# First q projection moved ahead of the second chunk's layer norm, with the first chunk's norm split over two engines

## The chip, the cores and the metric

The kernel runs on one core of one Trainium2 chip. The metric is the device time of one execution in microseconds (us), the median of three runs. The core has a matrix engine (PE; its weight loads are shown apart as PEld), a vector engine (VectorE, DVE in the profile), a scalar engine (ScalarE, ACT), GpSimd (POOL), and a sync engine (SP) that queues most of the transfers. All take their instructions in a fixed order that was decided when the kernel was built.

## The reference

The input x has 2048 tokens of 1024 features. It is normalized per token, then goes through a local attention (32 heads of 32, 8 keys at a distance of 2) and through a gated MLP, and both are combined with x:

```python
xn = _layernorm(x)                         # (x - mean) / sqrt(var + 1e-5), per token
qkv = xn @ wqkv                            # 1024 -> 3 x 1024: q, k, v
logits[w] = q[s] . k[s - 2 w] * Dh**-0.5   # w = 0..7
s = (softmax(logits) @ v[s - 2 w]) @ wo
g = silu((silu(xn @ w1) * (xn @ w3)) @ w2) # 1024 -> 3584 -> 1024
out = x + s * g
```

Data are bf16.

## The kernel before

The tokens are worked on in four chunks of 512 (CH), two chunks to a block (BL = 1024). A chunk is four tiles of 128 tokens. Each is loaded with tokens on partitions, normalized, and transposed by PE against an identity matrix; the transposed tiles are copied from PSUM into xT, which holds two chunks. The projections and the MLP read xT. The MLP's products are done by a scheme with sums of blocks (`xn_sums`, `w_sums`), which needs xT of both chunks of a block.

The norm comes in two forms. `ln_norm` takes the statistics on DVE and only the square root on ACT; `ln_norm_act` does the sums, squares and the scaling on ACT and only two tiny operations on DVE. In the kernel before, the first form serves block 0, the second block 1:

```python
def ln_norm(c, sts, xt4):
    ...
    for i, st in enumerate(sts):
        nc.sync.dma_start(out=xt4[:, st, :], in_=x_flat[g * P:(g + 1) * P, :])
        for h in range(2):
            nc.vector.bn_stats(out=stats[:, h, :], in_=xt4[:, st, h * 512:(h + 1) * 512])
        nc.vector.bn_aggr(out=mv[:, i, :], in_=stats[:])
    nc.scalar.activation(out=rstd[:], in_=mv[:, :, 1], func=ACTF.Sqrt, bias=eps_t[:], scale=1.0)
    nc.vector.reciprocal(out=rstd[:], in_=rstd[:])
    for i, st in enumerate(sts):
        nc.vector.tensor_scalar(out=xt4[:, st, :], in0=xt4[:, st, :], scalar1=mv[:, i, 0:1],
                                scalar2=rstd[:, i:i + 1], op0=ALU.subtract, op1=ALU.mult)

def ln_norm_act(c, sts, xt4):
    ...
    for i, st in enumerate(sts):
        nc.sync.dma_start(out=x_t, in_=x_flat[g * P:(g + 1) * P, :])
        nc.scalar.activation(out=junk[:], in_=x_t, func=ACTF.Copy, scale=-1.0 / D, accum_out=v[:, 0, i:i + 1])
        nc.scalar.activation(out=junk[:], in_=x_t, func=ACTF.Square, bias=v[:, 0, i:i + 1], accum_out=v[:, 1, i:i + 1])
    nc.scalar.activation(out=v[:, 2], in_=v[:, 1], func=ACTF.Sqrt, bias=eps_t[:], scale=1.0 / D)
    with tc.high_priority():
        nc.vector.reciprocal(out=v[:, 2], in_=v[:, 2])
        nc.vector.tensor_mul(v[:, 3], v[:, 0], v[:, 2])
    for i, st in enumerate(sts):
        nc.scalar.activation(out=x_t, in_=x_t, func=ACTF.Identity, bias=v[:, 3, i:i + 1], scale=v[:, 2, i:i + 1])

def ln_tp(c, st, xt4):                       # 8 transposes and 2 copies for one tile
    for kh in range(2):
        tp = bank(f"tp{c}_{st}_{kh}")        # one of 8 PSUM banks
        for k in range(KH):                  # KH = 4
            nc.tensor.matmul(tp[:, k * P:(k + 1) * P], lhsT=xt4[:, st, kt * P:(kt + 1) * P], rhs=ident[:], ...)
        nc.scalar.copy(out=xT[:, c % 2, kh * KH:(kh + 1) * KH, st * P:(st + 1) * P], in_=tp[:]...)

def ln_transpose(c, group=2):
    xt4 = r8.tile([P, NST, D], BF16, tag="r8", name=f"x{c}")    # one of 6 buffers of 8 KB a partition
    for st0 in range(0, NST, group):
        ln_norm(c, range(st0, st0 + group), xt4)
        for st in range(st0, st0 + group):
            ln_tp(c, st, xt4)

def qkv(c):
    ...
    for t in range(3):                       # q, k, v
        for hf in range(2):
            wt = r8.tile([P, 4, D], BF16, tag="r8")
            nc.sync.dma_start(out=wt[:], in_=wqkv_r[:, hf * 4:(hf + 1) * 4, t * D:(t + 1) * D])
        for j in range(NJ):                  # 8 groups of 8 matmuls, 128x512 each
            ps = bank(f"qkv{c}_{t}_{j}")
            mm_prod(ps, ...)                 # reads xT[:, half], all 512 tokens
            with tc.high_priority():
                nc.scalar.copy(out=dst, in_=ps[:])

ln_transpose(0, group=1)
ln_transpose(1)
for b in range(NB):
    qkv(c0)                                  # c0 = 2 b
    ...
    xn_sums(); mlp_up(...); attention(c0); ...; qkv(c1); mlp_up(...); attention(c1); mlp_down(b); wo(c0)
```

At the very start, 12 matmuls on a tile of zeros keep PE busy while the first tile of x is on its way.

Of the kernel before, what the change touches and what calls it, by code (L numbers as in the profile page):

```python
# [1 line left out]

# [14 lines left out]
def kernel(  # L17
# [21 lines left out]
    nc = tc.nc  # L39
# [8 lines left out]
    NST = CH // P  # L48
# [67 lines left out]
    def mm_prod(ps, lhs, rhs, first):  # L116
        n = len(lhs)
        for k in range(n):
            nc.tensor.matmul(  # L119
                ps[:], lhsT=lhs[k], rhs=rhs[k], start=(first and k == 0),  # L120
                stop=(k == n - 1), skip_group_check=not first,
            )

    def bank(name):
        return psum.tile([P, CH], FP32, tag="mm", name=name)
# [13 lines left out]
    def ln_norm(c, sts, xt4):  # L139
        n = len(sts)  # L140
        mv = small.tile([P, n, nc.vector.BN_AGGR_DIM], FP32, tag="mv")
        rstd = small.tile([P, n], FP32, tag="rstd")
        for i, st in enumerate(sts):
            g = c * NST + st
            nc.sync.dma_start(out=xt4[:, st, :], in_=x_flat[g * P:(g + 1) * P, :])
            stats = small.tile([P, 2, nc.vector.BN_STATS_DIM], FP32, tag="stats")
# [6 lines that stand above are left out]
            nc.vector.tensor_scalar(  # L153
                out=xt4[:, st, :], in0=xt4[:, st, :], scalar1=mv[:, i, 0:1], scalar2=rstd[:, i:i + 1],
                op0=ALU.subtract, op1=ALU.mult,
            )
# [16 lines left out]
            x_t = xt4[:, st, :]  # L173
            nc.scalar.activation(out=x_t, in_=x_t, func=ACTF.Identity, bias=v[:, 3, i:i + 1], scale=v[:, 2, i:i + 1])

    def ln_tp(c, st, xt4):
        for kh in range(2):
            tp = bank(f"tp{c}_{st}_{kh}")
            for k in range(KH):
                kt = kh * KH + k  # L180
                nc.tensor.matmul(
                    tp[:, k * P:(k + 1) * P], lhsT=xt4[:, st, kt * P:(kt + 1) * P], rhs=ident[:],
                    start=(k == 0), stop=(k == KH - 1), skip_group_check=True,
                )
            nc.scalar.copy(
                out=xT[:, c % 2, kh * KH:(kh + 1) * KH, st * P:(st + 1) * P],
                in_=tp[:].rearrange("p (k t) -> p k t", k=KH),
            )

    def ln_transpose(c, group=2):  # L190
        xt4 = r8.tile([P, NST, D], BF16, tag="r8", name=f"x{c}")
        for st0 in range(0, NST, group):
            ln_norm(c, range(st0, st0 + group), xt4)
            for st in range(st0, st0 + group):
                ln_tp(c, st, xt4)

    def qkv(c):
        half = c % 2
        if c > 0:
            nc.gpsimd.tensor_copy(out=kT[:, :, 0:HALO], in_=kT[:, :, CH:CH + HALO])  # L200
            nc.gpsimd.tensor_copy(out=vT[:, :, 0:HALO], in_=vT[:, :, CH:CH + HALO])  # L201
        for t in range(3):
            wts = []
# [3 lines that stand above are left out]
                wts.append(wt[:].rearrange("p k (c j) -> p k j c", j=NJ))  # L207
            for j in range(NJ):
                ps = bank(f"qkv{c}_{t}_{j}")
                mm_prod(ps, [wts[kt // 4][:, kt % 4, j, :] for kt in range(KT)],  # L210
                        [xT[:, half, kt, :] for kt in range(KT)], True)
                if t == 0:
                    dst = qo[:, half, j, :]
                elif t == 1:
                    dst = kT[:, j, HALO:HALO + CH]
                else:
                    dst = vT[:, j, HALO:HALO + CH]
                with tc.high_priority():
                    nc.scalar.copy(out=dst, in_=ps[:])  # L219

    def tree(t, z, op):
        op(t[:], z[:, 0:4, :], z[:, 4:8, :])
        op(t[:, 0:2, :], t[:, 0:2, :], t[:, 2:4, :])
        op(t[:, 0:1, :], t[:, 0:1, :], t[:, 1:2, :])
# [61 lines left out]
    def xn_sums():  # L286

        k_1, k_2 = slice(0, KH), slice(KH, KT)
        with tc.high_priority():
            nc.vector.tensor_sub(xs[:, 0], xT[:, 1, k_1, :], xT[:, 0, k_1, :])  # L290
            nc.vector.tensor_sub(xs[:, 1], xT[:, 1, k_2, :], xs[:, 0])
            nc.vector.tensor_sub(xs[:, 2], xT[:, 1, k_2, :], xT[:, 1, k_1, :])
            nc.vector.tensor_sub(xs[:, 3], xT[:, 0, k_2, :], xs[:, 1])
# [7 lines left out]
    def flush():  # L301
        while pend:
            pend.pop(0)()
# [101 lines left out]
    def w2_load(i):  # L405
        nc.sync.dma_start(out=w2_quarters(i).rearrange("p (a c) n -> p a c n", a=2), in_=w2_q[:, i])
# [15 lines left out]
    def mlp_down(b):  # L422
# [81 lines left out]
        for st in range(NST if b + 1 < NB else 0):  # L504
            ln_tp(2 * b + 2, st, xn[0])
# [7 lines left out]
        for st in range(NST if b + 1 < NB else 0):  # L513
            ln_tp(2 * b + 3, st, xn[1])
# [7 lines left out]
    def wo(c):  # L522
        u = c % 2
        gt = gts[u]
        for dh in range(2):
            wot = r8.tile([P, NJ, CH], BF16, tag="r8")
            nc.sync.dma_start(out=wot[:], in_=wo_r[:, :, dh * CH:(dh + 1) * CH])
            cols = slice(dh * CH, (dh + 1) * CH)
            for st in range(NST):
                g0 = (c * NST + st) * P  # L530
                ps = bank(f"s{c}_{dh}_{st}")
                mm_prod(ps, [qo[:, u, j, st * P:(st + 1) * P] for j in range(NJ)],
                        [wot[:, j, :] for j in range(NJ)], True)
                x_e = k2.tile([P, 2, CH], BF16, tag="k2")
                nc.sync.dma_start(out=x_e[:, 0], in_=x_flat[g0:g0 + P, cols])
                o_t = k2.tile([P, CH], FP32, tag="k2")
                with tc.high_priority():
                    nc.vector.tensor_mul(o_t[:], ps[:], gt[:, dh * NST + st])  # L538
                    nc.vector.tensor_add(x_e[:, 1], o_t[:], x_e[:, 0])  # L539
                    nc.scalar.dma_start(out=out_flat[g0:g0 + P, cols], in_=x_e[:, 1])  # L540

    cut = (11, 10)
    ln_transpose(0, group=1)
    ln_transpose(1)
    for b in range(NB):
        c0, c1 = 2 * b, 2 * b + 1
        qkv(c0)
        if b == 0:
            w2_load(0)
        else:  # L550
            wo(c0 - 1)
        xn_sums()
        mlp_up(b, range(cut[b]))
        attention(c0)
        flush()
        qkv(c1)
        mlp_up(b, range(cut[b], FB))
        flush()
        attention(c1)
        mlp_down(b)  # L560
        wo(c0)
# [31 lines left out]
```

## Time and profile before

| | |
|---|---|
| median of 3 runs | 779.67 us (778.84 to 781.32) |
| span of the profiled execution | 777.5 us |
| PE busy | 750.1 us (96%), 3457 matmuls |
| DVE busy | 602.0 us (77%) |
| ACT busy | 319.6 us (41%) |
| granted PE clock, mean | 0.982 |
| first q matmul | 21.74 us |
| first k matmul | 37.58 us |

How to read the profile: "busy" is the time in which an engine has at least one instruction under way. The page gives shares over the whole span, and under them the span in 40 slices with a digit for the busy tenths of each. For a change that touches the first tens of microseconds the whole-span shares say little; the same numbers for short windows, the timeline of single instructions, and the chain of work that ended last say more. The clock column is the share of PE's full clock that was granted. In names such as tp_2_0_180 the first two numbers are the token tile and the half of the features, the last only a running number; qkv_0_3 is q's fourth group, qkv_1 is k and qkv_2 is v. x_125 is the x buffer of chunk 0, x_214 that of chunk 1. L181 is the line of the transposes, L185 that of their copies, L119 that of all other matmuls, L148 to L153 the norm on DVE, L166 to L174 the norm on ACT.

### The profile page before, as it was taken

The numbers are of one execution on the slowest core, as the hardware profiler recorded it, in microseconds if no ns is written. First come the engines' busy times: TensorE is split into PE (matmuls) and PEld (weight loads), VectorE is DVE, ScalarE is ACT, GpSimd is POOL, SyncE is SP. The second block draws the span as 40 slices with busy tenths as digits, with TensorE's granted clock in tenths as the row PEclk, the third lists the DMA queues.
The fourth block names the chain that finished last, engine by engine and source line by source line (L and its number), as shares of the span: only waits on it lengthen the run. The fifth ranks groups of instructions, "written<-read, shape, count | busy, mean of one in ns | idle before, by whom it ended". The sixth has DMA issues, their size and how long they took to land.

```text
span 777.5 us, 9339 instructions
## 1 busy us (share of the span) xinstructions
PE 750.1 (96%) x3457; PEld 377.0 (48%) x3516; DVE 602.0 (77%) x829; ACT 319.6 (41%) x531; POOL 97.2 (12%) x172
## 2 busy tenths in 40 slices
PE   5999999999799999999999989999999999999997
PEld 3665444444365444445466434444456544444443
DVE  7249997896999899341599999474995995934997
ACT  4335444464134479456033045464433444221200
POOL 0000024124000000504000002221000004040000
PEclk7899999999999999999999989999999999999999
DMA  9362679889835395748863634756554347564634
GB/s 330 109 196 69 212 237 326 275 252 320 301 134 161 125 316 196 216 159 249 283 187 118 217 118 163 223 152 192 150 162 168 130 143 201 184 176 162 188 105 141
DMA packets 123117, 150.56 MB, mean 194 GB/s; under 512 B 6080, under 2 KB 97728, under 8 KB 119488
## 3 DMA queue, kind: packets, MB, share of 16 engines
q1 hardware_dynamic: 110336, 115.36, 47.8%
q0 software_dynamic: 8128, 30.42, 11.6%
q10 hardware_dynamic: 4608, 4.20, 1.6%
q8 instruction: 27, 0.44, 0.2%
q14 instruction: 18, 0.15, 0.1%
HBM read 115.34 MB, written 26.21 MB: 182 GB/s over the span
## 4 chain that ended last, share of the span: by engine, by line
PE 90%; DVE 4%; DMA 4%; issue 1%; ACT 1%; SPq 0%; ACTq 0%; DVEq 0%
DMA wt<-in_A_wqkv_dram 2%; PE db_0_2645 L119 1%; PE db_2_5575 L119 1%; PE db_3_2654 L119 1%; PE db_1_5572 L119 1%; PE db_2_2651 L119 1%; PE db_3_5578 L119 1%; PE db_0_5569 L119 1%; PE db_1_2648 L119 1%; DVE stats L148 1%; PE da_2_5539 L119 1%; PE da_0_5509 L119 1%; PE de_1_2876 L119 1%; PE de_2_5819 L119 1%; PE de_1_5800 L119 1%
## 5 line engine op out<-in xcount | busy, mean ns | idle before, releaser
L119 PEld LDWEIGHTS <-wt 128*128 128x128 bf16 x768 | 110.3, 144 | 64.9 <-DMA wt<-in_A_wqkv_dram 6.5
L119 PEld LDWEIGHTS <-h_sb 128*128 128x128 bf16 (+1 forms) x672 | 65.4, 98 | 78.0 <-issue 1.0
L233 DVE TENSOR_TENSOR p_t<-qo,kT 128x2048 bf16<-128x2048 bf16 x64 | 77.8, 1220 | 26.2 <-ACT kT L219 26.2
L119 PEld LDWEIGHTS <-qo 128*128 128x128 bf16 x256 | 25.0, 98 | 30.2
L235 DVE TENSOR_TENSOR p_t<-p_t 128x2048 bf16<-128x2048 bf16 x32 | 39.0, 1219 | 0.0
L269 DVE TENSOR_TENSOR B<-E,vT 128x2048 bf16<-128x2048 bf16 x32 | 38.8, 1219 | 0.0
L284 DVE TENSOR_TENSOR qo<-qo,B 128x2048 bf16<-128x2048 bf16 x24 | 29.3, 1222 | 0.4
L283 DVE TENSOR_TENSOR B<-B,C 128x2048 bf16<-128x2048 bf16 x24 | 29.4, 1226 | 0.1
L269 DVE TENSOR_TENSOR C<-E,vT 128x2048 bf16<-128x2048 bf16 x24 | 29.2, 1218 | 0.0
L539 DVE TENSOR_TENSOR x_e<-o_t,x_e 128x512 bf16<-128x512 f32 x32 | 21.7, 687 | 2.3 <-DMA x_e<-in_A_x_dram 1.8
L201 POOL COPY vT<-vT 128x128 bf16<-128x128 bf16 x3 | 3.5, 1170 | 152.6 <-DVE C L269 152.6
L236 DVE TENSOR_TENSOR p_t<-p_t 128x1024 bf16<-128x1024 bf16 x32 | 22.0, 687 | 0.2
L269 DVE TENSOR_TENSOR qo<-E,vT 128x2048 bf16<-128x2048 bf16 x8 | 9.7, 1218 | 15.8 <-DMA E<-pb_5434 15.8
L119 PEld LDWEIGHTS <-xT 128*128 128x128 f16 x112 | 11.0, 98 | 13.2
L417 POOL DMA_DIRECT2D t_dram<-w2q x14 | 7.6, 541 | 55.7 <-DVE w2q L416 55.7
L261 POOL DMA_DIRECT2D E<-pb_5434 x16 | 9.2, 580 | 36.4 <-DVE pb_5434 L258 34.0
L237 DVE TENSOR_TENSOR E<-p_t 128x512 bf16<-128x512 bf16 x32 | 13.4, 420 | 0.1
L261 POOL DMA_DIRECT2D E<-pb_4658 x16 | 9.2, 598 | 27.6 <-DVE pb_4658 L258 26.6
L261 POOL DMA_DIRECT2D E<-pb_2460 x16 | 9.2, 580 | 27.1 <-DVE pb_2460 L258 27.1
L538 DVE TENSOR_TENSOR o_t<-s_0_0_3163,xs 128x512 f32<-128x512 f32 x1 | 0.7, 692 | 15.3 <-PE s_0_0_3163 L119 15.3
L241 POOL DMA_DIRECT2D L_0_5402<-E x8 | 4.6, 584 | 53.3 <-DVE E L237 52.2
L200 POOL COPY kT<-kT 128x128 bf16<-128x128 bf16 x3 | 3.0, 1017 | 65.0 <-DVE p_t L233 54.5
(1484 smaller groups left out, 1742.3 us busy)
## 6 DMA issues: line engine op xcount, KB each, us to landing
wt<-in_A_wqkv_dram SPq DMA_DIRECT2D x24, 1024.0 KB, 7.0
wt<-t_dram SPq DMA_DIRECT2D x16, 896.0 KB, 5.6
wt<-in_B_w_dram SPq DMA_DIRECT2D x12, 896.0 KB, 6.0
wot<-in_A_wo_dram SPq DMA_DIRECT2D x8, 1024.0 KB, 7.9
w2q<-in_B_w_dram SPq DMA_DIRECT2D x14, 512.0 KB, 3.8
t_dram<-w2q POOLq DMA_DIRECT2D x14, 512.0 KB, 4.3
x_e<-in_A_x_dram SPq DMA_DIRECT2D x32, 128.0 KB, 2.7
out_dram<-x_e ACTq DMA_DIRECT2D x32, 128.0 KB, 2.6
```

The lines of the kernel that those rows point to most:

```text
L119: nc.tensor.matmul(ps[:], lhsT=lhs[k], rhs=rhs[k], start=(first and k == 0), stop=(k == n - 1), skip_group_check=not first,)
L148: nc.vector.bn_stats(out=stats[:, h, :], in_=xt4[:, st, h * 512:(h + 1) * 512])
L233: nc.vector.tensor_mul(p_t[:], qT[:, jh * 4:jh * 4 + 4, :], kT[:, jh * 4:jh * 4 + 4, o:o + CH])
L235: nc.vector.tensor_add(pr[0][:], pr[0][:], pr[1][:])
L236: nc.vector.tensor_add(pr[0][:, 0:2, :], pr[0][:, 0:2, :], pr[0][:, 2:4, :])
L237: nc.vector.tensor_add(E[:, w, :], pr[0][:, 0, :], pr[0][:, 1, :])
L261: nc.gpsimd.dma_start(out=E[r:P:NR, :, sq * P:(sq + 1) * P], in_=pb[sq * 32:(sq + 1) * 32, :, :],)
L269: nc.vector.tensor_mul(dst, E[:, w, :].unsqueeze(1).to_broadcast([P, 4, CH]), vT[:, js, o:o + CH])
L283: nc.vector.tensor_add(B[:], B[:], C[:])
L284: nc.vector.tensor_add(A, A, B[:])
L417: nc.gpsimd.dma_start(out=t_dram[:, i], in_=tq)
L539: nc.vector.tensor_add(x_e[:, 1], o_t[:], x_e[:, 0])
```

## The change

The change has two parts.

- Order: `ln_transpose(1)` is no longer called ahead of `qkv(0)`, but from inside it, after the q projection's instructions have been given. So the q weights are queued ahead of chunk 1's x, and q's 64 matmuls stand ahead of chunk 1's 32 transposes on PE. Its purpose is that q, which reads chunk 0 alone, need not wait for chunk 1.
- Sharing: in chunk 0 the token tile 2 is normalized by `ln_norm_act`, the other three by `ln_norm`, and the two copies of token tile 3 from PSUM go to DVE instead of ACT. Its purpose is that the two engines work on chunk 0 at once. All norms of a chunk are now given ahead of all its transposes.

```diff
-    def ln_tp(c, st, xt4):
+    def ln_tp(c, st, xt4, copy=nc.scalar.copy):
 ...
-            nc.scalar.copy(
+            copy(
                 out=xT[:, c % 2, kh * KH:(kh + 1) * KH, st * P:(st + 1) * P],
 ...
-    def ln_transpose(c, group=2):
+    def ln_transpose(c, group=2, fast=False):
         xt4 = r8.tile([P, NST, D], BF16, tag="r8", name=f"x{c}")
         for st0 in range(0, NST, group):
-            ln_norm(c, range(st0, st0 + group), xt4)
-            for st in range(st0, st0 + group):
-                ln_tp(c, st, xt4)
-
-    def qkv(c):
+            (ln_norm_act if fast and st0 == 2 else ln_norm)(c, range(st0, st0 + group), xt4)
+        for st in range(NST):
+            ln_tp(c, st, xt4, nc.vector.tensor_copy if fast and st == NST - 1 else nc.scalar.copy)
+
+    def qkv(c, mid=None):
 ...
                 with tc.high_priority():
                     nc.scalar.copy(out=dst, in_=ps[:])
+            if t == 0 and mid is not None:
+                mid()
 ...
-    ln_transpose(0, group=1)
-    ln_transpose(1)
+    ln_transpose(0, group=1, fast=True)
     for b in range(NB):
         c0, c1 = 2 * b, 2 * b + 1
-        qkv(c0)
+        qkv(c0, partial(ln_transpose, 1) if b == 0 else None)
```

As built, the changed kernel has the same number of instructions on PE and DVE, and on every engine the same order as before from the k projection on.

More of the change, by code (lines that the diff above doesn't have):

```diff
@@ L1 @@
 from contextlib import ExitStack, nullcontext
+from functools import partial
 import concourse.bass as bass
```

## The prediction

> **What bounds the kernel now.** I read four views in this order: the page's 40 slices (which engine is full where), the table of short windows over the first 30 us, the chain that ended last over the same stretch, and the timeline of single instructions. The slices first; each digit is a slice of 19.4 us.
>
> ```profile
> PE   5999999999799999999999989999999999999997
> DVE  7249997896999899341599999474995995934997
> ACT  4335444464134479456033045464433444221200
>
> ```
>
> PE is at 9 nearly everywhere; the page's chain is 90% PE. The first slice is one of the few holes: PE 5, clock 7. So whatever lets PE start its dense work earlier should come off the end, one for one, unless another engine takes over. The windows say what the hole is made of (columns: PE, weight load, DVE, ACT, POOL, clock, DMA share, GB/s):
>
> ```profile
> core 0: us, PE busy (x) PEld busy (x) DVE busy (x) ACT busy (x) POOL busy (x), PEclk, DMA share, GB/s
> 0.00:5.00 5.00, 3.78 (x9) 1.35 (x10) 1.89 (x5) 1.49 (x2) 1.42 (x10) 1.00 0.61 161
> 5.00:10.00 5.00, 2.67 (x20) 1.47 (x18) 5.00 (x14) 2.11 (x5) 0.00 (x0) 0.88 1.04 392
> 10.00:15.00 5.00, 1.89 (x16) 1.63 (x16) 4.93 (x14) 3.25 (x9) 0.00 (x0) 0.50 1.05 389
> 15.00:20.00 5.00, 1.89 (x16) 1.62 (x16) 2.56 (x9) 2.24 (x5) 0.00 (x0) 0.50 1.05 387
> 20.00:25.00 5.00, 4.72 (x23) 3.02 (x25) 3.16 (x4) 2.05 (x4) 0.00 (x0) 0.50 0.73 216
> ```
>
> From 5 to 15 us DVE is full: it is the layer norm of chunk 0 and, mixed into it, that of chunk 1. PE has only 16 small transposes per 5 us, and its clock has fallen to 0.50. DMA is full at 390 GB/s. The chain shows who releases whom (start, duration, what):
>
> ```profile
> 12.08 0.62 PE tp_2_0_180 L181 x4
> ...
> 12.73 2.05 ACT xT L185 x4
> ...
> 16.98 2.05 ACT xT L185 x4
> ...
> 20.06 0.61 PE tp_2_0_271 L181 x4
> ...
> 22.59 2.77 PE qkv_0_0_299 L119 x6
> ```
>
> The copy of 12.73 ends at 14.8 and completes chunk 0's xT. All that the first q projection needs is then there except, perhaps, weights. Yet it starts only at 21.74 (timeline), because chunk 1's transposes, in front of it on PE, wait until 20 us for their layer norm. That is about 7 us of idle PE for something the q projection doesn't read.
>
> [...]
>
> **Part 1: q in front of chunk 1.** As built, PE's new order is 32 transposes of chunk 0, 64 q matmuls, 32 transposes of chunk 1, then k; the rest is the same in order. Chunk 1's 32 transposes are not removed. They move behind q, where the clock is full: in the warm state the timeline has tp_0_0 at 7.14 and tp_0_1 at 7.37, so 4 take 0.23 us, 32 take **1.83 us**, now wholly on PE's path. q itself takes 37.58 - 21.74 = **15.84 us** from its first matmul to k's first, including a cold start of about 2 us (8 matmuls warm are 1.73 us, 64 are 13.8). I keep it unchanged: PE is just as cold in the new version.
>
> Are chunk 1's inputs ready when q ends? Its loads are now behind the two q weights. Bytes: 4 x tiles 1.05 MB, q weights 2.10 MB, 4 x tiles 1.05 MB. The windows give 0.8 MB moved by 5 us and 390 GB/s after: x of chunk 0 by 5.7, q weights by 8.3 and 11.0, x of chunk 1 by 13.7 us; landing about 0.6 later (the first x tile: 0.26 MB moved by about 2.8, statistics at 3.44). Then DVE needs about 8 statistics of 0.57 and 4 normalizations of 0.45, with small ones about 7 us: near 22 us. This is hidden under q.
>
> **Part 2: chunk 0's norm shared, when is xT ready?** DVE loses the 2 statistics of x tile 2 and all of chunk 1's from this stretch. ACT gets x tile 2: Copy, Square, Identity. Their costs are seen in the kernel's later use of the same function:
>
> ```profile
> 282.96 1.04 ACT L166 ACTIVATE junk_0_2538<-x_2535 128x1024 bf16<-128x1024 bf16 x1
> 283.90 0.19 ACT L166 ACTIVATION_READ_ACCUMULATOR junk_0_2538<-x_2535 128x1 f32 x1
> ...
> 285.04 1.13 ACT L167 ACTIVATE junk_0_2538<-x_2535,v 128x1024 bf16<-128x1024 bf16 x1
> 286.07 0.19 ACT L167 ACTIVATION_READ_ACCUMULATOR junk_0_2538<-x_2535,v 128x1 f32 x1
> ```
>
> Start to start this is 1.04 for Copy and 1.13 for Square with its read; Identity (x_2535, L174) follows at 1.13 to 1.23. No second activation table load is in the built order. That order on ACT is: Copy, square root of x0, Square, root of x1, root of x2, root of x3, Identity, then 6 copies of xT. Step by step, in us:
> - x2 lands near 5.6 (0.79 MB moved by 5.0, plus 0.6). Copy 5.6 to 6.65. The root for x0, ready at 5.4, stands behind it: 6.65 to 6.95.
> - DVE normalizes x0 about 7.7 (was 6.55). Square ends 8.0, roots of x1 and x2 until 8.5; DVE then forms the reciprocal and shift for x2 between its other work, until about 9.2.
> - Identity 9.25 to 10.4. PE transposes x2 at 10.5 and x3 until 12.2, at half clock (8 take 0.85).
> - ACT copies from 10.4 with a pitch of 0.48 (12.73 to 13.21 above in the timeline): the fifth starts at 12.3 and ends at 12.9, the sixth ends at 13.4. DVE's two for x3, from 12.0, 0.6 apart, end near 13.3; their first half by 12.7.
>
> The first four matmuls of q read the first half only, so q starts at **13.0** (was 21.74). So q is 8.7 us earlier, of which only 14.8 - 13.0 = 1.8 come from sharing the norm; the move makes the rest.
>
> **Sum.** k starts at 13.0 + 15.84 + 1.83 = 30.7 (was 37.58): **6.9 us** earlier. All later instructions keep their order, so I take the shift through to the end: 779.67 - 6.9 = **772.8 us**, 0.9%.
>
> **Rivals.**
> 1. *ACT becomes the bound at the start.* Its queue is strict: Copy waits for x2, and the roots behind it are held. It now has 3.3 us of x2 work ahead of six copies. If x2 lands 1 us later, or waits between DVE and ACT add up, q starts at 14 to 15, and sharing buys nothing: 774 to 775. For it: the chain of 6 to 8 hand-overs. Against it: DVE would have needed the time itself.
> 2. *Weights arrive last.* The second q weight lands near 11.6 and is needed by the fifth matmul, at 14.7. [...] If it failed, PE would wait 1 to 2 us: 774 to 775.
> 3. *DVE takes the end.* Chunk 1's xT copies now end at 28.85 + 0.7 + 8 x 0.48 = about 33.5, and the sums of xT (22.30 to 27.06 in the timeline, 4.8 us) end at 38.3. The attention product waits for k and would start at 30.7 + 7.7 = 38.4: a tie, where before DVE idled 18 us. Later slices have DVE at 9. But in the old timeline DVE idles 4.2 us after the first product, so a slip of a few us is absorbed. If not: 774.
> 4. *The start is hidden anyway*, because a transfer or DVE later sets the time: 779. Against it: PE is all but gapless from q to 197 us, and later waits hang on buffers that PE itself frees.
> 5. *A better clock.* Denser work might release the throttle earlier in q, up to 1 us: 771.8.
>
> **Range and chances.** The gain is bounded: it cannot exceed the 8.7 us less the transposes plus a better clock by much, about 8.5. Rivals 1 to 3 each take 1 to 2 us, seldom together; the runs of before spread over 2.5 us. That gives 770.3 to 775.6. Two per cent would be 15.6 us, more than the whole hole up to q's start less the work in it; so same is nearly certain.
>
> **What would show it.** Right: q's first matmul at 12.5 to 14, with the last xT copy of ACT its releaser; no wait of PE between q, the transposes and k; the transposes about 1.8 us; k at 30 to 31.5; from there the same timeline, shifted by some 7 us. Wrong in step 1: PE waits in front of chunk 1's transposes for DVE. Wrong in step 2: q at 14.5 or later, or a release by a weight DMA. Wrong in the sum: k is earlier by 7 us but the first MLP matmul, or the second chunk's q near 203 us, is not; then DVE or a load has taken the gap.

## The result and the profile after

The changed kernel takes **769.27 us** (median of 4 runs, 765.38 to 770.52), the kernel before 779.25 in the same session: a ratio of 0.986, interval 0.9819 to 0.9901. The prediction was 772.8 with a range of 770.3 to 775.6; the result lies 1 us under the range. In later sessions the changed kernel gave ratios of 0.9901 (0.9871 to 0.9931) and 0.9899 (0.9873 to 0.9925). All runs of the study together have medians of 778.2 for before (56 runs) and 769.5 for after (14 runs), so the gain is 8.7 us. Single runs of either scatter with a standard deviation of 1.7 us, which matters for what follows.

The windows over the first 25 us of the changed kernel, in the same columns as those of before (PE, weight load, DVE, ACT, POOL, clock, DMA share, GB/s):

```profile
0.00:5.00 5.00, 3.78 (x10) 1.44 (x11) 1.93 (x5) 1.49 (x2) 1.41 (x10) 1.00 0.59 191
5.00:10.00 5.00, 2.22 (x19) 1.54 (x17) 4.41 (x15) 3.71 (x9) 0.00 (x0) 0.82 1.02 358
10.00:15.00 5.00, 4.18 (x25) 2.65 (x24) 2.81 (x5) 3.52 (x7) 0.00 (x0) 0.50 1.05 395
15.00:20.00 5.00, 5.00 (x24) 3.29 (x23) 3.81 (x10) 1.95 (x4) 0.00 (x0) 1.00 1.05 387
20.00:25.00 5.00, 5.00 (x24) 3.30 (x23) 2.19 (x7) 1.79 (x4) 0.00 (x0) 1.00 0.38 140
```

From 15 us on PE is full, where before it had 1.89 of 5. The clock column holds the surprise: full from 15 us on, where before it stood at 0.50 up to 25 and beyond. PE's timeline (start, duration, instruction, count, and the idle time before it with its releaser) shows the new start:

```profile
8.49 1.89 PE L182 MATMUL tp<-ident,x 128*128 128x128 bf16 x16 [2.78 <-DVE x L154]
10.67 1.89 PE L182 MATMUL tp<-ident,x 128*128 128x128 bf16 x16 [0.29 <-ACT x L175]
13.08 14.90 PE L120 MATMUL qkv<-xT,wt 128*128 128x512 bf16 x64 [0.52 <-ACT xT L186]
27.82 1.95 PE L182 MATMUL tp<-ident,x 128*128 128x128 bf16 x32
29.61 10.75 PE L120 MATMUL qkv<-xT,wt 128*128 128x512 bf16 x49
```

q starts at 13.08, released by ACT's copies of xT; chunk 1's 32 transposes run at 27.82 without a wait; k starts at 29.61, 7.97 us ahead of 37.58. The span is 766.9 us against 777.5, so 10.6 us less, which says that this pair of traces gains 2.6 us more after k's start. DVE has 828 instructions in the profile, one fewer than the 829 before, so the number there is not quite the same as I had said.

### The profile page after: what moved, and what is told of

Read it like the earlier page. It is cut to its first block, busy times and chain, and to the rows that moved or that the text cites. A ratio compares the mean times of both kernels' runs of the same rounds, so it can differ in the third digit from the quotient of the medians.

```text
span 766.9 us, 9404 instructions
## 1 busy us (share of the span) xinstructions
PE 749.4 (98%) x3516; PEld 375.6 (49%) x3516; DVE 602.1 (79%) x828; ACT 321.1 (42%) x534; POOL 97.2 (13%) x172
## 4 chain that ended last, share of the span: by engine, by line
PE 86%; DVE 8%; DMA 4%; issue 1%; ACT 1%; SPq 0%; DVEq 0%; ACTq 0%
PE ub L120 18%; PE qkv L120 15%; PE ue L120 12%; PE ua L120 12%; PE db L120 9%; PE de L120 6%; PE da L120 6%; PE s L120 5%; DMA wt<-in_A_wqkv_dram 2%; DVE B L286 1%; DVE B L272 1%; DVE qo L287 1%; DVE p_t L236 1%; PE tp L182 1%; DVE C L272 1%
## 5 line engine op out<-in xcount | busy, mean ns | idle before, releaser
L120 PE MATMUL qkv<-xT,wt 128*128 128x512 bf16 x768 | 169.9, 383 | 4.9 <-DMA wt<-in_A_wqkv_dram 4.4
L120 PEld LDWEIGHTS <-st 128*128 128x128 f16 x896 | 87.7, 98 | 107.4 <-issue 1.7
L120 PE MATMUL ua<-xT,w 128*128 128x512 bf16 x448 | 106.7, 381 | 2.9 <-ACT ub L131 2.9
L120 PEld LDWEIGHTS <-w 128*128 128x128 bf16 x672 | 65.9, 98 | 84.0 <-issue 5.9
L120 PE MATMUL ub<-xs,st 128*128 128x512 f16 x448 | 106.7, 381 | 0.0
L120 PE MATMUL db<-wt,h_sb 128*128 128x512 f16 x336 | 73.7, 379 | 0.0
L120 PE MATMUL s<-wot,qo 128*128 128x512 bf16 x256 | 55.7, 379 | 0.0
L120 PE MATMUL ub<-xs,w 128*128 128x512 f16 x224 | 53.4, 379 | 0.9 <-DVE h_sb L383 0.9
L120 PE MATMUL ue<-xs,st 128*128 128x512 f16 x224 | 52.9, 379 | 0.1
L120 PE MATMUL ue<-xT,st 128*128 128x512 bf16 x224 | 52.9, 379 | 0.0
```

What stands on the lines that cost most here:

```text
L120: nc.tensor.matmul(ps[:], lhsT=lhs[k], rhs=rhs[k], start=(first and k == 0), stop=(k == n - 1), skip_group_check=not first,)
```

## The experiments

**Two theories.** The order theory: moving q is the change, its gain is fixed at k's first matmul, and all after it is shifted. The sharing rival: splitting chunk 0's norm is what shortens the start. For the missing gain: the clock theory, that PE loses less time at half clock, against a gain in later waits brought on by the earlier start.

**The order alone.**

```diff
-            (ln_norm_act if fast and st0 == 2 else ln_norm)(c, range(st0, st0 + group), xt4)
-        for st in range(NST):
-            ln_tp(c, st, xt4, nc.vector.tensor_copy if fast and st == NST - 1 else nc.scalar.copy)
+            ln_norm(c, range(st0, st0 + group), xt4)
+            for st in range(st0, st0 + group):
+                ln_tp(c, st, xt4)
```

> Only the move of q ahead of chunk 1; chunk 0 is normalized as in the kernel before (DVE alone, copies on ACT). Theory (the order is the change): q's first matmul at 13.5 to 14.5 us (changed kernel 13.08, before 21.74), k's first at 30 to 31.5 (changed 29.61), so 7 us or more of the 8 us by which k came earlier; median about 770 to 772.5. Rival (the sharing is needed, because DVE alone holds chunk 0 back): q no earlier than 14.8, median 773 or more.

Measured: 770.58 us, ratio 0.9917 (0.9894 to 0.9941). PE's timeline of this kernel:

```profile
11.32 1.89 PE L182 MATMUL tp<-ident,x 128*128 128x128 bf16 x16 [1.72 <-DVE x L154]
13.58 15.05 PE L120 MATMUL qkv<-xT,wt 128*128 128x512 bf16 x62 [0.37 <-ACT xT L186]
```

q starts at 13.58, only half a microsecond after the changed kernel, and k at 30.26 (in this kernel each tile's transposes follow its norm again, as before). The first of the two lines tells why DVE alone is nearly as fast: the last sixteen transposes start at 11.32, against 12.08 before, as DVE no longer mixes chunk 1's statistics into chunk 0's.

**The sharing alone.**

```diff
-    qkv(c0, partial(ln_transpose, 1) if b == 0 else None)
+    ln_transpose(1)          # ahead of the loop again
+    qkv(c0)
```

> Only the sharing of chunk 0's norm; chunk 1's loads, norm and transposes stay ahead of q. Theory: q still waits for chunk 1's transposes; first q matmul at 19.5 to 21.5 (before 21.74), median 777.5 to 779.5. Rival (sharing the norm is what shortens the start): q before 18, median below 776.

Measured: 777.54 us, ratio 0.9993 (0.9977 to 1.0008). q's first matmul is at 21.15, in line with the theory. The sharing rival falls: by itself it is worth nothing that can be measured, and on top of the order 0.5 us of q's start, too little to tell in the medians.

**The kernels themselves again.** No edit; for more times and traces.

> The changed kernel once more, unaltered, for the spread and for a second trace. [...] Rival (the later gain is a fixed effect of the earlier start): the shift grows from 8 to 10.5 again at the same places.

> The changed kernel, unaltered, for a third trace and more times. Theory: q's first matmul at 13.0 to 13.5, k at 29.5 to 31 depending on where the clock's half-rate stretch ends (15.0 and 17.3 us in the two traces so far); median 769 to 771. Rival (the first trace is typical, the clock always recovers at 15 us): k at 29.6 within 0.2.

> The kernel before, unaltered, for a second trace. Theory (the first trace of before was an unlucky one late in its run: it has two half-clock windows at 449 us where all four variants have one, and a DVE sum holds the loads of the next q at 197 us): k's first matmul again at 37 to 38.5 us, but the later shift of about 2 us against the variants shrinks to under 1 us. Rival (the shift after k is an effect of the change): this trace repeats the first one at 195 to 207 and 449 to 456 us within 0.5 us.

> The kernel before, unaltered, for a third trace; the same theory and rival as for the second.

Measured: the changed kernel 769.68 and 769.30 us; the kernel before 778.43 and 778.19 (one run each). The three traces of each kernel put the pieces side by side (us; means in the last column):

| | three traces | mean |
|---|---|---|
| before: q's first matmul | 21.74, 21.93, 21.74 | 21.80 |
| after: q's first matmul | 13.08, 13.42, 12.94 | 13.15 |
| before: q's duration, to k | 15.84, 15.26, 15.01 | 15.37 |
| after: q's duration, to the transposes | 14.74, 15.72, 13.81 | 14.76 |
| after: the transposes, to k | 1.79, 1.79, 1.79 | 1.79 |
| before: k's first matmul | 37.58, 37.19, 36.75 | 37.17 |
| after: k's first matmul | 29.61, 30.93, 28.54 | 29.69 |
| before: k to the end | 739.9, 739.5, 739.7 | 739.7 |
| after: k to the end | 737.3, 737.9, 738.5 | 737.9 |

q's start varies little; its duration varies by 1.9 us in one and the same kernel. The clock column shows why: two windows over 12 to 20 us, first of the second trace of the changed kernel (q 15.72 us),

```profile
12.00:16.00 4.00, 3.25 (x15) 1.76 (x14) 3.50 (x7) 1.85 (x4) 0.00 (x0) 0.50 1.05 391
16.00:20.00 4.00, 4.00 (x16) 2.31 (x16) 1.70 (x6) 1.37 (x3) 0.00 (x0) 0.83 1.05 386
```

then of the third (q 13.81 us):

```profile
12.00:16.00 4.00, 3.35 (x18) 2.31 (x18) 3.97 (x8) 1.96 (x4) 0.00 (x0) 0.98 1.05 389
16.00:20.00 4.00, 4.00 (x20) 2.68 (x19) 3.57 (x10) 1.36 (x3) 0.00 (x0) 1.00 1.05 388
```

In the third the clock is back at 1.00 at 12.1 us, before q starts at 12.94; in the second it stays at 0.50 up to 17.3 us, nearly 4 us into q. In the first traces the stretches at half clock lasted 17.07, 3.41 and 6.83 us in before (from 8.78, 203.3 and 449.1 us) and 6.83, 3.41 and 3.41 us in after (from 8.17, 195.9 and 441.7 us), apart from the one in which the run ends. So the rival that the clock always recovers at 15 us falls, and my own range for k (29.5 to 31) was missed by the third trace, with 28.54. But so does my guess that the first trace of before was an unlucky one after k: its other two traces need as long from k to the end, so the 1.8 us of the last two rows are no accident of one trace.

**PE kept busy at the start.** The changed kernel with 18 extra matmuls on the tile of zeros, each into a bank that the next instruction overwrites. They change no result.

```diff
+    def fill(ps, n):
+        for _ in range(n):
+            nc.tensor.matmul(ps[:], lhsT=warm[:, 0:P], rhs=warm[:], start=True, stop=True)
 ...
             tp = bank(f"tp{c}_{st}_{kh}")
+            if c == 0 and kh == 0:
+                fill(tp, FILL[st])                 # FILL = (10, 1, 3, 0, 4)
 ...
                 ps = bank(f"qkv{c}_{t}_{j}")
+                if c == 0 and t == 0 and j == 0:
+                    fill(ps, FILL[NST])
```

> The changed kernel with 18 extra matmuls on the tile of zeros (10 ahead of the first tile's transposes, 1 and 3 ahead of the second's and third's, 4 ahead of q), each in the bank that the next instruction overwrites, to keep PE busy while chunk 0 is normalized. Theory (the cold clock of PE costs about 1 us in q and some tenths in the transposes): the clock stays 1.00 from 5 us on, q's first matmul at 12.6 to 13.1, q's first group of 8 takes 1.75 us instead of 2.7, k at 28 to 28.8 (changed 29.61); 1 to 1.5 us less than the changed kernel. Rival (the copies on ACT alone set the start, and the clock does not matter, or the extra matmuls delay the transposes): k at 29.5 or later, no gain.

Measured: 767.58 us, ratio 0.9885 (0.9853 to 0.9917). The clock is 1.00 up to 193 us (the mean over the span is 0.997, against 0.990 in the changed kernel's first trace); q starts at 13.46, no earlier than without filling, and lasts 13.81 us to the transposes; k starts at 29.06. So the part on q's duration holds, the parts on q's start and on k don't (12.6 to 13.1 and 28 to 28.8 had been expected). ACT sets q's start. Its scaling of token tile 2 (Identity) starts at 9.38 us in the changed kernel and at 9.75 in the filled one:

```profile
9.38 1.24 ACT L175 ACTIVATE x<-x,v 128x1024 bf16<-128x1024 bf16 x1 [0.49 <-DVE v L172]
9.75 1.24 ACT L175 ACTIVATE x<-x,v 128x1024 bf16<-128x1024 bf16 x1 [0.38 <-DVE v L172]
```

From there to q's first matmul, over the six copies, it is 3.70 us at half clock and 3.71 at full clock. The Identity is later in the filled kernel's trace because DVE waited 1.06 us for a tile of x, against 0.52 in the changed kernel's. Against the changed kernel's median the step is 1.9 us, though the intervals overlap.

**The copies split over two engines.** The filled kernel, with token tiles 0 and 1 copied by DVE and 2 and 3 by ACT, and the first half of the features transposed first (3 extra matmuls ahead of q instead of 4).

```diff
-        for st in range(NST):
-            ln_tp(c, st, xt4, nc.vector.tensor_copy if fast and st == NST - 1 else nc.scalar.copy)
+        for khs in ((0,), (1,)) if fast else ((0, 1),):
+            for st in range(NST):
+                ln_tp(c, st, xt4, nc.vector.tensor_copy if fast and st < 2 else nc.scalar.copy, khs)
```

> The changed kernel with 17 extra matmuls on zeros to keep PE busy, as before, and with chunk 0's eight copies from PSUM split by token tile (tiles 0 and 1 on DVE, 2 and 3 on ACT) and transposed first half of the features first, so that the six copies of ACT no longer stand between the norm and q. Theory (after the clock, the copies on ACT set q's start): q at 12.2 to 12.8, k at 28.0 to 28.6, about 0.5 to 1 us less than the kernel with extra matmuls alone (k 29.06, median 767.58), so near 766.5 to 767. Rival (norm or x's landing sets it): q at 13.3 or later, no gain over that kernel.

Measured: 767.72 us, ratio 0.9884 (0.9859 to 0.9909). In its trace q starts at 11.95 and k at 27.55, 1.5 us ahead of the filled kernel's, but the median is no lower. Half of the 1.5 us is luck: x landed earlier, and the Identity starts at 8.97, 0.78 us earlier. From there to q it is 2.98 us instead of 3.71, so the split copies are worth 0.7 us at k. At the end they drown in what the later stretches at half clock take: this trace has half-rate stretches of 6.8 us at 191 us and 3.4 us at 440 us, where that of the filled kernel has one of 3.4 us at 193 us; the mean clocks are 0.992 and 0.997.

**No cold window anywhere.** PE has two more holes, near 200 us (the second chunk's q waits for its weights) and near 447 us (the second block's MLP waits for a copy by ACT). They too were filled, in the kernel before, in the changed kernel and in the one with split copies: 16 matmuls on zeros ahead of q of chunk 1, and a product that is computed anyway repeated. The kernel before also got 40 matmuls on zeros at its start.

```diff
             for i in I:
                 pe.append(bank(f"ue{b}_{fl[i]}"))
-                mm_prod(pe[i], s1[i], t1, True)
+                for _ in range((3, 2)[i] if b == 1 and fb == 0 else 1):
+                    mm_prod(pe[i], s1[i], t1, True)
```

> The kernel before with PE kept busy in all its holes by matmuls that change nothing: 40 on zeros while both chunks of block 0 are normalized, 16 on zeros ahead of the second chunk's q (each in a bank that the next instruction overwrites), and at the start of block 1's MLP three and two times, instead of once, the same first product of the sums. No half-clock window is left, or one. Theory (a part of the gain of the change, 1 to 2 us, is clock, not order): q at 20.8 to 21.5, k at 34.7 to 35.4 (before 37), median 770.5 to 773. Rival (the clock is of no account in the holes, PE waits there anyway): median 775 or more.

> The changed kernel with the 18 extra matmuls at its start and the same two later fillings as in the other two. Theory: k at 28.3 to 29.1, so 6 to 6.7 us ahead of the filled kernel before, and nearly the same distance, up to 1.2 us more, at the end: median 764 to 766, the two filled kernels 6 to 8 us apart. Rival (the gain after k has nothing to do with the clock): the two are 8.5 us apart or more, and their traces differ in the waits at 195 and 445 us by 2 us.

> The kernel with the split copies and all fillings. Theory: q at 11.8 to 12.5, k at 27.4 to 28.2, 0.8 to 1.5 us ahead of the filled changed kernel, median 763 to 765. Rival (no cold window left to save, copies not on the path): equal to the filled changed kernel within 0.3 us.

Measured: 772.32 us (ratio 0.9936, 0.9919 to 0.9953) for the filled kernel before; 766.32 us (0.9857, 0.9837 to 0.9878) for the filled changed kernel; **765.94 us** (0.9849, 0.983 to 0.9867) for the filled one with split copies. The last beats both kernels, by 3.6 us the changed one's 769.5; it can't be told from the filled changed kernel, and it missed the 763 to 765 that I expected. The single times of the filled kernel before lie within 1.2 us, those of the unfilled one in the same session within 3.8; the filled changed kernel still scatters by 2.9 (765.05 to 766.32 in three runs with a clock of 1.00, 767.93 and 767.98 in two with 0.997). Two lines of the timelines, filled kernel before first,

```profile
19.27 1.06 PE L187 MATMUL tp<-ident,x 128*128 128x128 bf16 x16
20.16 20.03 PE L119 MATMUL qkv<-xT,wt 128*128 128x512 bf16 x90
```

then filled changed kernel:

```profile
14.16 13.97 PE L120 MATMUL qkv<-xT,wt 128*128 128x512 bf16 x63 [0.49 <-ACT xT L192]
27.97 1.95 PE L188 MATMUL tp<-ident,x 128*128 128x128 bf16 x32
```

Sixteen transposes now take 1.06 us where the cold ones took 1.89, and q takes 13.81 us.

The medians of the filled pair are 6.0 us apart, within the 6 to 8 that I expected; those of the unfilled pair are 8.7 apart. But the difference of 2.7 us is no measure of the clock, because the filled pair differs in more than the clock:

- As built, the filled kernel before has another order on DVE and ACT at its start: chunk 1's last two tiles are normalized at 17.07 us, in the kernel before at 19.45. So q starts at 20.16 instead of 21.80 for two reasons, warm transposes and this order, which no run separates.
- In the trace of the filled changed kernel a tile of x landed late: ACT's first work on it starts at 6.85 us, against 5.80 in the changed kernel's first trace. q starts at 14.16, a whole microsecond later than without filling.

At k the filled pair is therefore only 4.2 us apart (33.98 and 29.76; the first is taken from the first MLP matmul at 61.62, which comes 27.64 us after k in the unfilled traces of both kernels). I had expected 6 to 6.7. After k the filled changed kernel gains another 1.8 us (734.8 against 736.6 to the end), although the clock is at 1.00 in both from k on up to 764 us (the means over the spans are 0.999 and 1.000). So **a gain of this size after k needs no difference in clock**; on this point the rival is right, though neither its 8.5 us nor the waits that it named came about. The longest waits of PE after k, filled kernel before first:

```profile
PE da L119 <- DMA wt<-in_B_w_dram: 2.0, 1, 2.0
PE ua L119 <- ACT ub L130: 1.8, 1, 1.8
```

then filled changed kernel:

```profile
PE ua L120 <- ACT ub L131: 1.5, 1, 1.5
```

The 2.0 us are a wait of `mlp_down`'s first product (da) for its weights, 0.1 us in the filled changed kernel; why that load is late stays open.

## Why the prediction was wrong

The start was right nearly to the tenth:

- *q's start*: predicted 13.0, measured 13.08 (12.94 to 13.42), with ACT's copies as releaser. ACT's way there too: Copy at 5.80 (predicted 5.6), Identity at 9.38 (9.25), copies from 10.52 (10.4). The order on ACT held as rival 1 has it: the root for x0, whose input DVE had finished at 5.38, started only at 6.85, behind the Copy that had waited for x2.
- *Chunk 1's transposes*: predicted 1.83 us at full clock, measured 1.79. Their inputs were ready; PE didn't wait.
- *No stall by weights, DVE or chunk 1's norm*: rivals 1 to 4 did not come about in the three traces of the changed kernel. (Rival 1 did in the filled one's: x a microsecond later, q at 14.16.) The landing times in the prediction take it that loads are served in the order in which they are queued. No run shows that as a rule; in the changed kernel's first trace the loads did land in that order, x of chunk 0 from 3.3 to 6.4 us, the q weights at 10.1 and 12.8 (expected near 8.9 and 11.6) and x of chunk 1 from 13.4 to 15.5 (expected by 14.3), later than I had put them, without a wait of PE.

What failed:

1. **The step "q itself takes 15.84 us ... I keep it unchanged: PE is just as cold in the new version".** It measured 14.74, 15.72 and 13.81 us: on average 1.1 us less than assumed. Of this, 0.5 us is that 15.84 was the longest of before's three (mean 15.37), and 0.6 is gain that I missed. The clock accounts for all six durations. By the clock column q ran at 0.50 for 4.1, 2.9 and 2.4 us in before and for 1.9, 3.9 and 0 us in after; half of that on top of the 13.81 us at full clock gives 15.9, 15.3, 15.0 and 14.8, 15.8, 13.8. What PE did at half clock at the start differs too. In before's first trace it paused between the transposes and was busy for 10.4 of the 17.07 us (3.25 of them in the last 3.41 us, mostly with q). In after the transposes of chunk 0 stand closer together (8.49 to 12.56 with one gap) and q follows 0.5 us later: in the first trace PE was busy for 5.7 of the 6.83 us. In these two traces the clock was back sooner where PE was busier. But with the same order of work it was back at 17.3 us in the second trace and at 12.1 us, before q, in the third. Why, the traces don't show; I take it for luck. My rival 5 named this, with up to 1 us and as a mere chance. It belonged into the sum, and its scatter (1.9 us in three traces of one kernel) into the range.

2. **The step "I take the shift through to the end".** This is the larger miss. Between k's first matmul and the end the changed kernel takes 1.8 us less (737.9 against 739.7, means of three traces). It was not a shift of one and the same course, as the waits at the two later holes show. The waits of PE, kernel before first (engine, waiting, awaited: total us, times, longest):

```profile
PE qkv_0_0_1831 L119 <- DMA wt<-in_A_wqkv_dram: 4.4, 1, 4.4
PE ua_0_3677 L119 <- ACT ub_0_3697 L130: 3.4, 1, 3.4
```

and the changed kernel:

```profile
PE qkv L120 <- DMA wt<-in_A_wqkv_dram: 4.4, 3, 3.5
PE ua L120 <- ACT ub L131: 2.9, 1, 2.9
```

The longest wait for q's weights fell from 4.4 to 3.5 us (4.2 and 5.1 in before's other traces, 3.6 and 3.5 in after's). Those loads stand in SP's queue right behind a load into the w2 buffer, which waits until a write out of that buffer has landed (SP's wait for it took 10.5 us in before, 10.1 in after); before first, then after:

```profile
196.70 0.37 SPq L406 DMA_DIRECT2D w2q<-in_B_w_dram  x1
197.18 2.15 SPq L206 DMA_DIRECT2D wt<-in_A_wqkv_dram  x3
```

```profile
187.89 0.37 SPq L409 DMA_DIRECT2D w2q<-in_B_w_dram  x1
188.35 3.00 SPq L207 DMA_DIRECT2D wt<-in_A_wqkv_dram  x3
```

The write issued last ahead of this hole took 6.7, 6.4 and 7.3 us to land in before, 5.8, 5.8 and 5.9 in after. Counted from k, the second chunk's q starts after 165.9 us in before and 164.9 us in after (means of three). So about 1.0 of the 1.8 us stands in that wait. Another 0.5 us stands in the wait at the second hole, PE for a copy by ACT: 3.4, 4.1 and 3.1 us in before, 2.9, 2.6 and 3.3 in after. The stretches at half clock in the two holes add up to 10.2 us in each trace of before, to 6.8, 10.2 and 10.2 in those of after; they can be the rest, but not the main part, since half of the difference of their means is 0.6 us. What shortens the write is not the earlier start: the kernel with the sharing alone has 6.0 us, with k at 37.05 us hardly earlier than before (37.17), and takes 737.9 us from k to the end like the changed kernel. The cause **stays open**.

3. **The base.** I subtracted from 779.67, the median of three runs. Over 56 runs the kernel before has 778.2. So of the 3.3 us between 772.8 and 769.5, 1.8 are gain that I missed and 1.5 are a base that was too high. (The first two points sum to 2.4 us; the three traces of each kernel are 9.3 us apart at the end, 0.6 us more than the medians, which is within the scatter.)

4. **The 1.8 us put down to sharing.** I took 14.8, the end of chunk 0's copies before, for what DVE alone would need. But there DVE had statistics of chunk 1 mixed in. Without them q starts at 13.58, so sharing gave 0.5 us, and the move the rest. This left the sum alone but gave the wrong part the credit.

## What to carry to other kernels

Work that an engine can start on should not stand in its fixed order behind work whose inputs come later: here 64 matmuls went in front of 32 transposes and started 8.7 us earlier. Where a trace shows PE at half clock in the stretch that the change makes denser, count that time as a term of the sum, with its scatter from several traces (here 1.9, 3.9 and 0 us of q in three traces of one kernel), and not as a constant. Filling PE's holes takes it out of a comparison only where the other engines keep their order, so compare the orders too. A shift at the start need not arrive at the end unchanged: here a later wait for a load changed by 1.0 us. Before subtracting a gain of under 1%, know the base from more than three runs.

## What the runs showed of the hardware

- In the three traces of the changed kernel the stretch at half clock at the start ended at 15.0, 17.3 and 12.1 us, and q took 14.74, 15.72 and 13.81 us. In all six traces of the two kernels q's duration is within 0.1 us of 13.81 us plus half of the time that it ran at a clock of 0.50.
- Matmuls on zeros, which nothing reads, kept the clock at 1.00 (18 at the start, up to 193 us; 34 in all, and 12 of a repeated product, in the filled changed kernel, up to 764 us). The times were 1.9 us less with the start alone, and 3.2 us less in all (769.5 to 766.3).
- In the first traces PE's waits of 4.4 and 3.4 us in before were followed by 3.41 and 6.83 us at half clock, those of 3.5 and 2.9 us in after by 3.41 us each. The two filled kernels, with waits of 2.0 us and less after k, had a clock of 1.00 from k up to 764 us.
- The same 512 KB write took 6.4 to 7.3 us to land in three traces of before, 5.8 to 5.9 in three of after, 5.9 with the order alone and 6.0 with the sharing alone, without a cause that these runs show.
